# Grouped-query attention and a gated MLP on one core: idle matmuls with a bank of their own or not, normalisation without a DVE wait for the root, first-batch scores in pairs

## The chip, the core and the metric

The kernel runs on one NeuronCore of a Trainium2 chip. The core has a matrix engine (TensorE, PE in the profile; its weight loads are shown apart as PEld), and the engines VectorE (DVE), ScalarE (ACT), GpSimd (POOL) and SyncE (SP, which here issues transfers). Each engine runs its own queue strictly in the order written; they meet through semaphores. PE writes its results into PSUM, which has eight banks of 512 float32 values per partition. The metric is the device time of one execution in microseconds: 253.52 us before the change, the median of three runs (253.1, 253.52 and 254.39).

## What is computed

Attention over 8 batches with 16 query heads, 4 key/value heads, 384 positions and 64 values per head; its output goes as x (384 x 1024 per batch) into a gated MLP. The scores are so small that the kernel leaves out the subtraction of the maximum.

```python
scores = scale * np.matmul(q, k.transpose(0, 1, 3, 2))
attn = softmax(scores)                      # over keys
x = np.matmul(attn, v)                      # heads side by side: 1024 columns
h = np.maximum(x @ w_in, 0.0)               # 1024 x 1024
u, v = h[..., :512], h[..., 512:]
v_n = (v - mean(v)) / np.sqrt(var(v) + 1e-06)
v_s = np.einsum('ts,bsd->btd', w_spatial, v_n) + b_spatial[None, :, None]
out = (u * v_s) @ w_out
```

## The kernel before

The order of every engine's work is written out by hand: one loop over steps n (L594), where each step issues some of the following, in this order.

- `todo` entries (L595): loads, and casts of q, k and v on POOL to float16; from batch 2 on also transposes by DMA from SP.
- Scores (L597 to L601). A unit is one third of the keys for one group of query columns; a batch has 18 units. `scores(n)` issues two matmuls of a 64-row operand each (L233) and one exponential on ACT over both results (L240). In steps 0 to 16 one unit is issued a step, one step ahead; from step 18 on two units in every even step. The tile sc has two buffers, so a unit needs the exponential of the unit before last to be done.
- `weigh` (L242): every three units, 12 short matmuls (L247, four query tiles by three key tiles) into the tile av, twice, one step after the other. av has one buffer. DVE then takes the reciprocal of the sums (L257) and multiplies (L259) into x16; the next av waits for that.
- `turns` entries (L606): transposes on PE in the first batches (kps L188, qps L200, xps L275, each followed by a copy on DVE), and `keep_warm(4)` in steps 0 to 9, 14 and 15: four matmuls of an identity whose result nobody reads (L504). 27, 4 and 6 more stand ahead of step 0.
- `run_fill`: matmuls of the MLP from one generator (`stream`, L424), as many columns as the step is due. In batch 0 it gives work in steps 10 to 13 and from 16 on, none in 14 and 15. The MLP of a batch runs while the attention of the next one is issued; v_tile (pv, L294), u_tile or u_block (pu, L344 or L361), gate (psp, L380) and project (po, L406).

The tiles of the transposes, of the MLP and of the idle matmuls (`warm`) share the tag "ck" with three PSUM banks; sc takes four banks and av one. A ck tile takes the bank that was free longest; before the change `warm` is one tile that is made once (L500) and used last in step 15, so up to there the other ck tiles go round two banks, and a tile waits until the copy of the tile two before it is done.

The normalisation of a batch (`normal`, L311) comes in the middle of its u matmuls. DVE has clipped v into vr (L304) and taken statistics and mean and variance (L306, L307). ACT takes the logarithm of the variance and an exponential of -0.5 times that (L314, L315), which is the reciprocal root `rstd`. DVE multiplies minus the mean by it (`nmr`, L316), and POOL computes vn = vr * rstd + nmr three times (L322). psp reads vn. In the last batch no other attention is left beside this.

Of the kernel before, what the change touches and what calls it, by code (L numbers as in the profile page):

```python
# [9 lines left out]
FP32 = mybir.dt.float32  # L10
FP16 = mybir.dt.float16
AF = mybir.ActivationFunctionType
ALU = mybir.AluOpType
# [4 lines left out]
def kernel(  # L18
# [16 lines left out]
    nc = tc.nc  # L35
    P = 128
# [5 lines left out]
    NT = S // P  # L42
# [6 lines left out]
    NU = 18  # L49
# [7 lines left out]
    small = ctx.enter_context(tc.tile_pool(name="small", bufs=4))  # L57
# [3 lines left out]
    ps_ck = ctx.enter_context(tc.tile_pool(name="ps_ck", bufs=3, space=PSUM))  # L61
# [29 lines left out]
    def load_q0(j, lo, hi, eng):  # L91
# [18 lines left out]
            name=nc.get_next_instruction_name(), act_func_set_id=set_id, ins=[], outs=[]  # L110
# [113 lines left out]
    def scores(n):  # L224
        b, r = divmod(n, NU)
        m, t = divmod(r, NT)
        qt, j = divmod(m, 2)
        if t == 0:
            aTs[b, m] = att.tile([P, NT, 2, 512], FP16, name=f"aT_{b}_{m}", tag="aT", bufs=3)
        sc = ps_sc.tile([P, 2, 512], FP32, name=f"sc_{b}_{m}_{t}", tag="sc")  # L230
        for hh in range(2):
            half = slice(hh * D, (hh + 1) * D)
            nc.tensor.matmul(  # L233
                sc[:, hh],
                kTs[b][half, j, t * P : (t + 1) * P],
                qTs[b, j][half, qt],
                start=True,
                stop=True,
            )
        nc.scalar.activation(aTs[b, m][:, t], sc, AF.Exp, scale=scale)  # L240

    def weigh(b, m, hh):  # L242
        qt, j = divmod(m, 2)
        av = ps_av.tile([P, G, D + 1], FP32, name=f"av_{b}_{m}_{hh}", tag="av")
        for i in range(G):
            for t in range(NT):
                nc.tensor.matmul(  # L247
                    av[:, i, :],
                    aTs[b, m][:, t, hh, i * P : (i + 1) * P],
                    v1[b % 2][:, 2 * j + hh, t, 0 : D + 1],  # L250
                    start=(t == 0),
                    stop=(t == NT - 1),
                )
        if m == 0 and hh == 0:
            x16s[b] = att.tile([P, NT, NB, P], FP16, name=f"x16_{b}", tag="x16")
        r = small.tile([P, G, 1], FP32, name=f"r_{b}_{m}_{hh}", tag="r")
        nc.vector.reciprocal(r, av[:, :, D : D + 1])  # L257
        blk = 4 * j + 2 * hh
        nc.vector.tensor_tensor(  # L259
            x16s[b][:, qt, blk : blk + 2].rearrange("p k (i d) -> p (k i) d", i=2),  # L260
            av[:, :, 0:D],
            r.to_broadcast([P, G, D]),
            ALU.mult,
        )
# [21 lines left out]
    mvs, v_rs, v_ns, uTs, gTs, osbs = {}, {}, {}, {}, {}, {}  # L286
# [23 lines left out]

    def normal(b):  # L311
        rstd = small.tile([P, NT], FP32, name=f"rstd_{b}", tag="rstd")
        nmr = small.tile([P, NT], FP32, name=f"nmr_{b}", tag="nmr")
        nc.scalar.activation(rstd, mvs[b][:, :, 1], AF.Ln, bias=eps_t)  # L314
        nc.scalar.activation(rstd, rstd, AF.Exp, scale=-0.5)  # L315
        nc.vector.scalar_tensor_tensor(  # L316
            nmr, mvs[b][:, :, 0], -1.0, rstd, op0=ALU.mult, op1=ALU.mult
        )
        v_ns[b] = []
        for st in range(NT):  # L320
            vn = moe.tile([P, DH], FP16, name=f"vn_{b}_{st}", tag="vn", bufs=6)
            nc.gpsimd.tensor_scalar(  # L322
                vn,
                v_rs[b][st],
                rstd[:, st : st + 1],
                nmr[:, st : st + 1],
                op0=ALU.mult,
                op1=ALU.add,
            )
            v_ns[b].append(vn)  # L330

# [5 lines left out]
    def u_tile(b, st):  # L337

        pu = ps_ck.tile([P, NM, P], FP32, name=f"pu_{b}_{st}", tag="ck")
        for m in range(NM):  # L340
            for kt in range(NB):
                if st == 1 and m == 1 and kt == 0:
                    normal(b)
                nc.tensor.matmul(  # L344
                    pu[:, m],
                    w_in16[:, kt, m * P : (m + 1) * P],
                    x_tile(b)[:, st, kt],
                    start=(kt == 0),
                    stop=(kt == NB - 1),
                )  # L350
                if m < NM - 1 or kt < NB - 1:
                    yield P
        nc.vector.tensor_scalar(
            uT_tile(b)[:, :, st * P : (st + 1) * P], pu, 0.0, None, op0=ALU.max
        )
        yield P

    def u_block(b, m):
        pu = ps_ck.tile([P, 512], FP32, name=f"pu_{b}_{m}", tag="ck")
        for kt in range(NB):  # L360
            nc.tensor.matmul(  # L361
                pu[:, 0:S].rearrange("p (t s) -> p t s", t=NT),
                w_in16[:, kt, m * P : (m + 1) * P],
                x_tile(b)[:, :, kt],
                start=(kt == 0),
                stop=(kt == NB - 1),
            )
            if m == 0 and kt == 3:
                normal(b)
            if kt < NB - 1:  # L370
                yield S
        nc.scalar.activation(uT_tile(b)[:, m, :], pu[:, 0:S], AF.Relu)
        yield S
# [123 lines left out]

    by_dve, by_act = nc.vector.tensor_copy, nc.scalar.copy

    warm = ps_ck.tile([P, 512], FP32, name="warm", tag="ck")  # L500

    def keep_warm(n):
        for _ in range(n):
            nc.tensor.matmul(warm[:, 0:P], ident16, ident16, start=True, stop=True)  # L504

    keep_warm(27)
    cast_k(0, dve, (0,))
    cast_q(0, 0, dve, 0, 1, by_act)
    k_transposes(0, 0, by_dve)
    keep_warm(4)  # L510
    q_transposes(0, 0, 0, by_act, by_dve)
    keep_warm(6)
    scores(0)
    cast_k(0, pool, (1,))
# [71 lines left out]
    total = NU * B  # L586

    def run_fill(cols):
        nonlocal owed
        owed += cols  # L590
        while owed > 0:
            owed -= next(fill, 1e9)

    for n in range(total + 6):  # L594
        for f, args in todo.pop(n, []):  # L595
            f(*args)
        if n + 1 < NU:  # L597
            scores(n + 1)
        elif n >= NU and n % 2 == 0 and n < total:
            scores(n)  # L600
            scores(n + 1)  # L601
        for hh in range(2):
            b, r = divmod(n - 3 - hh, NU)
            if n >= 3 + hh and r % 3 == 0 and b < B:
                weigh(b, r // 3, hh)
        for f, args in turns.pop(n, []):  # L606
            f(*args)
        if n < NU + 3:

            run_fill(HV / 4 if 10 <= n < 14 else 2 * HV / 5 if 16 <= n else 0)  # L610
        elif n < 2 * NU + 4:
            run_fill((4 * HV + NM * NT * S + 6 * NM * 512) / (NU + 4 - 3))
        else:
            run_fill(COLS / NU)
# [31 lines left out]
```

## Time and profile before

| what | value |
|---|---|
| time, median of 3 runs | 253.52 us (253.1 to 254.39) |
| profiled execution, its own time | 253.12 us |
| span of the profiled execution | 251.3 us |
| PE busy | 240.9 us (96%) |
| ACT busy | 168.2 us (67%) |
| DVE busy | 139.7 us (56%) |
| POOL busy | 98.3 us (39%) |
| DVE idle ahead of nmr (L316), in all 8 | 9.9 us |
| PE idle, all stretches | 10.4 us |

Times in the profile are microseconds from the start of the span. A row of a timeline gives start, length, engine, line of the kernel, operation, tile written <- tiles read, shapes, and how many instructions are merged; a bracket names the idle time of that engine just before, and what ended it. Matmuls overlap in PE's pipeline, so the length of a row reaches past the start of the next one; what a piece of work costs PE is read from start to start. A row by stretch gives the busy time and number of instructions of PE, PEld, DVE, ACT and POOL, the granted clock, the busy share of the DMA engines and GB/s.

The matmuls run on PE at two speeds: the four idle matmuls at 4.80 us take 0.43 us start to start, those from 8.36 us on 0.22 to 0.24 us where no change to the 64-row form of the scores follows.

### The profile page before, as it was taken

The page shows a single profiled execution, that of the slowest core. Times are in us where ns is not written, and L with a number is a line of the kernel's source. Part 1 is how long each engine was busy: PE and PEld are TensorE (multiplying, and loading weights), DVE is VectorE, ACT ScalarE, POOL GpSimd, SP SyncE. Part 2 cuts the span into 40 slices and gives each one's busy share as a digit, 9 for nine tenths or more (in the row PEclk, how much of TensorE's full clock was granted, in tenths as well). Part 3 has the DMA queues.
Part 4 walks back from the last instruction along what each step waited for, and adds up shares of the span by engine and source line. Part 5 has one row for each costly group of instructions (what it writes and reads, how often), then busy time and mean ns, then how long its engine had stood idle before and what let it go on. Part 6 is the DMA issues. An engine that isn't in the chain of part 4 may idle for free.

```text
span 251.3 us, 6020 instructions
## 1 busy us (share of the span) xinstructions
PE 240.9 (96%) x2430; PEld 125.7 (50%) x2430; DVE 139.7 (56%) x368; ACT 168.2 (67%) x215; POOL 98.3 (39%) x142
## 2 busy tenths in 40 slices
PE   7898998999999999999999999999999999999883
PEld 7564657534455444544455445544455445544442
DVE  2455776854626755474626655474636655465462
ACT  3996566678696687768696687768696687741211
POOL 2698837871035701392036602391035003320320
PEclk9999999999999999999999999999999999999999
DMA  7999998999289964997399956997392452106006
GB/s 179 268 285 251 301 285 238 297 224 265 88 182 330 171 230 85 266 233 216 121 199 324 185 200 66 281 253 227 111 171 49 111 183 44 34 12 250 0 22 232
DMA packets 73981, 46.93 MB, mean 187 GB/s; under 512 B 48113, under 2 KB 68913, under 8 KB 73953
## 3 DMA queue, kind: packets, MB, share of 16 engines
q1 hardware_dynamic: 68832, 37.63, 59.4%
q0 software_dynamic: 4080, 8.65, 13.8%
q8 instruction: 19, 0.31, 0.5%
q10 hardware_dynamic: 1040, 0.26, 0.5%
q14 instruction: 10, 0.07, 0.1%
HBM read 25.95 MB, written 12.58 MB: 153 GB/s over the span
## 4 chain that ended last, share of the span: by engine, by line
PE 87%; DVE 7%; issue 1%; ACT 1%; POOL 1%; POOLq 0%; DVEq 0%
PE av L247 17%; PE pv L294 16%; PE sc L233 15%; PE po L406 15%; PE pu L361 13%; PE psp L380 6%; PE warm L504 3%; DVE stats L306 2%; DVE vr L304 2%; DVE x L259 2%; PE pu L344 1%; PE qps L200 1%; ACT aT L240 1%; POOL vn L322 1%; PE xps L275 1%
## 5 line engine op out<-in xcount | busy, mean ns | idle before, releaser
L240 ACT ACTIVATE aT<-sc 128x1024 f16<-128x1024 f32 x144 | 139.6, 1021 | 52.9 <-PE sc L233 52.7
L247 PEld LDWEIGHTS <-aT 128*128 128x128 f16 x1152 | 43.4, 97 | 32.9 <-DVE x L259 12.9
L322 POOL TENSOR_SCALAR vn<-vr,rstd,nmr 128x512 f16<-128x512 f32 x24 | 18.1, 767 | 99.6 <-DVE r L257 85.7
L247 PE MATMUL av<-v,aT 128*128 128x65 f16 x1152 | 52.3, 194 | 1.6 <-DVE x L259 1.2
L294 PE MATMUL pv<-w_in,xt 128*128 128x512 f16 x192 | 49.5, 378 | 0.0
L257 DVE RECIPROCAL r<-av 128x4 f32<-128x4 f32 x96 | 17.1, 178 | 58.3 <-PE av L247 57.8
L406 PE MATMUL po<-w_out,gT 128*128 128x512 f16 (+1 forms) x196 | 48.2, 375 | 0.9 <-POOL gT L392 0.9
L233 PE MATMUL sc<-qT,kT 64*128 64x512 f16 x288 | 45.0, 382 | 0.7 <-ACT aT L240 0.4
L259 DVE TENSOR_TENSOR x<-av,r 128x256 f16<-128x256 f32 x96 | 40.7, 424 | 3.4
L361 PE MATMUL pu<-xt,w_in 128*128 128x384 f16 x224 | 41.7, 326 | 0.0
L392 POOL TENSOR_TENSOR gT<-g,uT 128x384 f16<-128x384 f32 x30 | 26.5, 914 | 29.4 <-DVE g L390 29.4
L361 PEld LDWEIGHTS <-w_in 128*128 128x128 f16 x224 | 20.2, 97 | 14.7 <-issue 2.5
L406 PEld LDWEIGHTS <-gT 128*128 128x128 f16 x196 | 17.0, 97 | 19.4 <-issue 2.9
L170 POOL CAST q<-q 128x768 f16<-128x768 f32 (+1 forms) x36 | 24.9, 732 | 3.1 <-DMA q<-in_q_dram 3.1
L415 DVE COPY osb<-po 128x512 f32<-128x512 f32 (+1 forms) x25 | 16.8, 671 | 11.6 <-PE po L406 11.6
L294 PEld LDWEIGHTS <-xt 128*128 128x128 f16 x192 | 16.2, 97 | 13.5 <-issue 0.7
L415 ACT COPY osb<-po 128x512 f32<-128x512 f32 (+1 forms) x24 | 13.9, 580 | 12.4 <-PE po L406 12.3
L304 DVE TENSOR_SCALAR vr<-pv 128x512 f32<-128x512 f32 x24 | 16.5, 687 | 10.2 <-PE pv L294 10.0
L233 PEld LDWEIGHTS <-kT 64*128 64x128 f16 x288 | 8.9, 94 | 26.6 <-issue 24.4
L380 PE MATMUL psp<-wsT,vn 128*128 128x384 f16 x96 | 19.6, 326 | 0.6 <-POOL vn L322 0.6
L390 DVE TENSOR_TENSOR g<-psp,bias_b 128x384 f32<-128x384 f32 x32 | 16.4, 552 | 5.9 <-PE psp L380 5.9
L306 DVE BATCH_NORM_STATS2 stats<-vr 128x6 f32<-128x512 f32 x24 | 16.7, 695 | 0.8
(49 smaller groups left out, 125.8 us busy)
## 6 DMA issues: line engine op xcount, KB each, us to landing
out_dram<-osb SPq DMA_DIRECT2D x21, 512.0 KB, 2.9
q<-in_q_dram SPq DMA_DIRECT2D x10, 768.0 KB, 7.2
q<-in_q_dram POOLq DMA_DIRECT2D x4, 768.0 KB, 10.4
v<-in_v_dram SPq DMA_DIRECT2D x6, 384.0 KB, 8.7
w_in<-in_moe_w_in_dram POOLq DMA_DIRECT2D x4, 512.0 KB, 9.7
k<-in_k_dram SPq DMA_DIRECT2D x5, 384.0 KB, 4.2
out_dram<-osb SPq DMA_DIRECT2D x5, 256.0 KB, 2.0
q<-in_q_dram SPq DMA_DIRECT2D x2, 512.0 KB, 7.2
```

The lines of the kernel that those rows point to most:

```text
L170: f(q16s[b, j][:, lo:hi, :, hh, :], src[:, hh, lo:hi])
L233: nc.tensor.matmul(sc[:, hh], kTs[b][half, j, t * P : (t + 1) * P], qTs[b, j][half, qt], start=True, stop=True,)
L240: nc.scalar.activation(aTs[b, m][:, t], sc, AF.Exp, scale=scale)
L247: nc.tensor.matmul(av[:, i, :], aTs[b, m][:, t, hh, i * P : (i + 1) * P], v1[b % 2][:, 2 * j + hh, t, 0 : D + 1], start=(t == 0), stop=(t ...
L259: nc.vector.tensor_tensor(x16s[b][:, qt, blk : blk + 2].rearrange("p k (i d) -> p (k i) d", i=2), av[:, :, 0:D], r.to_broadcast([P, G, D]) ...
L294: nc.tensor.matmul(pv, x_tile(b)[:, st, kt], w_in16[:, kt, DH:DFF], start=(kt == 0), stop=(kt == NB - 1),)
L306: nc.vector.bn_stats(stats, vr)
L361: nc.tensor.matmul(pu[:, 0:S].rearrange("p (t s) -> p t s", t=NT), w_in16[:, kt, m * P : (m + 1) * P], x_tile(b)[:, :, kt], start=(kt == 0 ...
L380: nc.tensor.matmul(psp[:, 0:S], v_ns[b][st][:, m * P : (m + 1) * P], wsT16[:, st, :], start=(st == 0), stop=(st == NT - 1),)
L392: by.tensor_tensor(gTs[b][:, m, :], g, uTs[b][:, m, :], ALU.mult)
L406: nc.tensor.matmul(po[:, 0 : hi - lo], gTs[b][:, m, tt * P : (tt + 1) * P], w_out16[:, m, lo:hi], start=(m == 0), stop=(m == NM - 1),)
L415: (nc.scalar.copy if half and not i else nc.vector.tensor_copy)(osb[:, lo:hi], po[:, 0 : hi - lo])
```

## The change

Three edits:

1. `keep_warm` makes a new `warm` tile at each call, of the same tag. Between calls its bank goes back to the three that the ck tiles use in turn. The number of idle matmuls stays 85.
2. vn = (vr + minus) * rstd, where `minus` is minus the mean. DVE computes it from the mean alone; POOL waits for DVE and for ACT. nmr is gone.
3. In batch 0, units 0 to 12 are issued as before, no unit in step 12, unit 13 in step 13, and 14 with 15 and 16 with 17 in steps 14 and 16. From step 18 on nothing moves.

```diff
     def normal(b):
         rstd = small.tile([P, NT], FP32, name=f"rstd_{b}", tag="rstd")
-        nmr = small.tile([P, NT], FP32, name=f"nmr_{b}", tag="nmr")
+        minus = small.tile([P, NT], FP32, name=f"minus_{b}", tag="minus")
         nc.scalar.activation(rstd, mvs[b][:, :, 1], AF.Ln, bias=eps_t)
         nc.scalar.activation(rstd, rstd, AF.Exp, scale=-0.5)
-        nc.vector.scalar_tensor_tensor(
-            nmr, mvs[b][:, :, 0], -1.0, rstd, op0=ALU.mult, op1=ALU.mult
-        )
+        nc.vector.tensor_scalar(minus, mvs[b][:, :, 0], -1.0, None, op0=ALU.mult)
         v_ns[b] = []
         for st in range(NT):
             vn = moe.tile([P, DH], FP16, name=f"vn_{b}_{st}", tag="vn", bufs=6)
             nc.gpsimd.tensor_scalar(
                 vn,
                 v_rs[b][st],
+                minus[:, st : st + 1],
                 rstd[:, st : st + 1],
-                nmr[:, st : st + 1],
-                op0=ALU.mult,
-                op1=ALU.add,
+                op0=ALU.add,
+                op1=ALU.mult,
             )
             v_ns[b].append(vn)
...
-    warm = ps_ck.tile([P, 512], FP32, name="warm", tag="ck")
-
     def keep_warm(n):
+        warm = ps_ck.tile([P, 512], FP32, name="warm", tag="ck")
         for _ in range(n):
             nc.tensor.matmul(warm[:, 0:P], ident16, ident16, start=True, stop=True)
...
-        if n + 1 < NU:
+        if n < 12:
             scores(n + 1)
-        elif n >= NU and n % 2 == 0 and n < total:
+        elif n == 13:
+            scores(n)
+        elif n % 2 == 0 and n > 13 and n < total:
             scores(n)
             scores(n + 1)
```

## The prediction

> **What bounds the kernel now.** I read the shares first, then the chain that ended last, then busy time by stretch, then single engines in order of time where TensorE (PE) was idle. The page's shares, its 40 slices and its chain:
>
> ```profile
> PE 240.9 (96%) x2430; PEld 125.7 (50%) x2430; DVE 139.7 (56%) x368; ACT 168.2 (67%) x215; POOL 98.3 (39%) x142
> PE   7898998999999999999999999999999999999883
> PE 87%; DVE 7%; issue 1%; ACT 1%; POOL 1%; POOLq 0%; DVEq 0%
> ```
>
> PE bounds the span; at most the idle 10.4 us and what hides inside groups counted as busy can be won. Busy time by stretch says where it idles:
>
> ```profile
> 20.00:25.00 5.00, 4.16 (x61) 2.41 (x58) 3.31 (x9) 3.19 (x5) 3.91 (x6) 1.00 1.17 234
> 35.00:40.00 5.00, 4.43 (x70) 3.06 (x67) 3.37 (x10) 3.37 (x6) 0.63 (x1) 1.00 1.05 332
> 121.00:149.00 28.00, 27.97 (x274) 13.64 (x272) 15.50 (x42) 20.82 (x27) 10.60 (x14) 1.00 0.83 204
> 235.00:240.00 5.00, 4.37 (x27) 2.34 (x25) 1.65 (x4) 1.52 (x5) 3.15 (x4) 1.00 0.02 3
> ```
>
> The second number is PE. A middle batch (121 to 149) leaves it 0.03 us; the first batch (0.84 and 0.57 us idle in these two stretches) and the end (0.63) leave more. In order of time, PE in the first batch:
>
> ```profile
> 19.36 0.39 PE L233 MATMUL sc<-qT,kT 64*128 64x512 f16 x2
> 20.07 0.39 PE L200 MATMUL qps<-ident,q 128*128 128x128 f16 x4
> 21.29 0.38 PE L275 MATMUL xps<-ident,x 128*128 128x128 f16 x4 [0.84 <-DVE qT L205]
> 26.71 1.67 PE L294 MATMUL pv<-w_in,xt 128*128 128x512 f16 x7
> 28.31 0.60 PE L233 MATMUL sc<-qT,kT 64*128 64x512 f16 x4
> 28.85 0.54 PE L247 MATMUL av<-v,aT 128*128 128x65 f16 x12
> ```
>
> Two things: xps waits for the copy of qT out of the bank that both use, and a pair of units costs 0.54 us start to start (28.31 to 28.85), a single one 0.32 (19.36 to 19.68). Next, DVE at the first batch's normalisation and in a middle batch, with the PE rows that hang on it:
>
> ```profile
> 39.10 0.16 DVE L316 SCALAR_TENSOR_TENSOR nmr<-mv,rstd 128x3 f32<-128x3 f32 x1 [0.60 <-ACT rstd L315]
> 39.87 0.55 PE L247 MATMUL av<-v,aT 128*128 128x65 f16 x12 [0.57 <-DVE x L259]
> 127.19 0.16 DVE L316 SCALAR_TENSOR_TENSOR nmr<-mv,rstd 128x3 f32<-128x3 f32 x1 [1.45 <-ACT rstd L315]
> 127.34 0.61 PE L233 MATMUL sc<-qT,kT 64*128 64x512 f16 x4
> 127.96 0.54 PE L247 MATMUL av<-v,aT 128*128 128x65 f16 x12
> ```
>
> While DVE waits for the root, the division of the weighted values (L257, L259) is queued behind it, and the one bank of av with it: PE loses 0.57 us once, and 0.62 - 0.54 = 0.08 us inside the pair at 127.34. Last, the end:
>
> ```profile
> 235.04 0.20 ACT L315 ACTIVATE rstd<-rstd 128x3 f32<-128x3 f32 x1
> 235.28 0.16 DVE L316 SCALAR_TENSOR_TENSOR nmr<-mv,rstd 128x3 f32<-128x3 f32 x1 [0.60 <-ACT rstd L315]
> 235.64 2.26 POOL L322 TENSOR_SCALAR vn<-vr,rstd,nmr 128x512 f16<-128x512 f32 x3 [13.84 <-PE pu L361]
> 237.96 0.82 PE L380 MATMUL psp<-wsT,vn 128*128 128x384 f16 x4 [0.41 <-POOL vn L322]
> ```
>
> Root, nmr, three vn and then PE, with nothing beside it.
>
> **Banks and pairs, first batch.** The same 85 idle matmuls are issued; their tile no longer holds one of three ck banks until step 15. The order of DVE, ACT, POOL and SP stays; on PE only the scores of units 13 to 17 move. In the built order qps of step 12 now takes the bank of an older qps, and xps that of an older xps whose copy ended at 18.0: nothing is left for xps to wait for. From step 16's query transposes on, each ck tile has the same predecessor in its bank as before. I walk PE from 19.25 (the pv pair at 18.82 takes 2 x 0.216) with start-to-start times of rows of before:
> - step 12: av 0.39, qps 0.22, xps 0.22, two pv 0.53: 20.61
> - step 13: unit 13 0.32, av 0.39, two pv 0.53: 21.85
> - step 14: units 14 and 15 0.54, four idle matmuls 0.24, kps 0.22: 22.85
> - step 15: av 0.39, idle 0.22, kps 0.22, qps 0.22, xps 0.32; step 16: units 16 and 17 0.54, av 0.39, qps 0.22: 25.37.
>
> Two stalls are new. The pair of step 14 has av of step 15 close behind, and no filling work between (the filler gives nothing in steps 14 and 15). ACT starts an exponential 0.43 after its unit (22.04 to 22.47), takes 1.02, and a waiting av goes on about 0.06 later (at 60.35 an av stretched to 0.64 resumed so after the exponential of 59.58). Unit 14 at 21.85 is ready at 23.30, its av resumes at 23.36 instead of 22.91: 0.45 lost. Unit 15 waits for the exponential of 13 (21.04 to 22.06) about 0.03. So pv of step 16 comes at 25.85, not 26.71: 0.86 gained. Bounds: the stall may be nothing (1.31 gained) or the whole 1.02 (0.29); I take the walk. Behind PE in that stall stand only transposes and scores, all of them in the walk; ACT, which feeds it, is not delayed.
>
> What is late next: the first u matmuls come at 28.8 instead of 29.67, and their weights, issued by POOL at 15.9 and 16.6 with at most 11.3 us to land, are there by 27.9. DVE's copies keep up: kT's copy starts 1.54 after vr (23.50 to 25.04) and vr now at 22.07, so the bank of step 15's qps is free at 23.95; qps comes at 24.16. POOL's casts for batch 2 come 1 us earlier and their loads (issued at 28.5 and 29.4, 13.1 and 13.9 to land) still lie ahead. SP's key and query transposes (from 46.87) follow an x of DVE at 41.1, which moves with PE.
>
> The new waits of PE for itself (a bank last written by an idle matmul) are long over but one: the second qps at 5.44 writes a bank whose idle matmul ends at 5.43. It heads the chain to the first exponential; 0 to 0.1, I take 0.05 lost.
>
> A rule speaks against the stall. PE idles 1.0 us from 20.29 to 21.29 in this trace, and the four xps after it still take 0.22 (21.29 to 21.51), as the four qps before it; 0.45 us should not slow the clock either. The Trainium skill ("TensorE: Matmul & The Clock Gate", Part 1) has the gate fall to half after about 3.4 us of idleness; by that too the stall costs its own length, and the trace's 1.0 us agrees.
>
> **DVE without the root.** Eight times nmr (160 ns) becomes minus, a one-input operation on 128x3; the nearest rows are nmr and a 59 ns fill, and the next instruction starts 0.08 after it (39.10 to 39.18), so between 0 and 0.08 counts; I take 0.08.
> - First batch: aggregation ends at 38.50, minus 38.53, reciprocal 38.61, x 38.82 to 39.24, av 39.30 instead of 39.87. PE's own work before it ends at about 39.14, so 0.57 is gained (at most 0.73, at least 0 if something else held DVE).
> - Middle batches: reciprocal can start when av of 125.89 is out, about 126.5 and not 127.27; then av follows the pair after 0.54. The same 0.62 stands in six batches (71.24, 99.29, 127.34, 155.40, 183.45, 211.50): 6 x 0.08 = 0.48. The bounds are 0 and 0.48.
> - Last batch: POOL waits for ACT (ends 235.24) directly. Hops in these rows are 0.04 to 0.20, so vn starts at 235.28 to 235.44 instead of 235.64: 0.20 to 0.36; I take 0.24. psp, g, gT and the projection hang on it in a row, so it reaches the end.
> - vn keeps its shape and two scalars: 767 ns, same price. Fourteen osb copies of DVE now name a wait for ACT that the root's wait used to cover; the ACT copy meant is four osb tiles old. A wait instruction takes 21 ns on DVE's queue: nothing if covered by DVE's idle time, 0.3 at worst.
>
> **Sum**: 0.86 + 0.57 + 0.48 + 0.24 - 0.05 = 2.10 us. The profiled execution took 253.12 us (span 251.3 and 1.8 around it): 251.0. The median of the runs shown is 0.40 above it; I take half of that and say 251.2.
>
> **Rivals.**
> - The first-batch time is taken back by a load or by ACT: then only DVE's part stays, 1.29 - 0.05: 251.9, with the offset 252.1. For: DMA share is 1.05 to 1.2 in these stretches and POOL waits for a w_in landing until 28.5. Against: the margins of 0.9 us above.
> - DVE's wait only moves (something else holds reciprocal, or PE's 0.08 is its own): gain 0.86 + 0.24 - 0.05 = 1.05: 252.1, with the offset 252.3. For: the 0.08 is inside a modelled group. Against: 0.57 is plain idle time.
> - Slower: the idle matmuls now go round three banks among waiting tiles, PE rests at each and its clock falls. At half clock (four idle matmuls take 0.43 at 4.80 to 5.23 and 0.22 later) the 19 us up to step 16 would lose up to 12: 263. It decides from 3.4 us of work done at half clock (2.1 + 1.3). Against: the transposes of before already cycle through two banks with no slow row after 6.8. The same page of the Trainium skill ("A second HAM failure mode: psum-queue depth-cycling") describes such a fall; the trace does not show it.
> - Banks don't change what xps waits for, so the edit does not do what it says: 0.86 turns to about -0.1, which is the first rival's time.
>
> **How the numbers follow.** Forecast 0.71; first rival with the last one 0.12; second 0.10; slower 0.07. Less than 0.5% (1.27 us) is about what this measurement can't tell from no change: the line is at 252.25. Below it lie 0.67 of the forecast (the runs shown spread by 1.3 us, so its tail does not) and 0.13 of the two middle cases: 0.80; within it the other 0.13; slower 0.07. The forecast's own range is 250.4 (all upper bounds) to 251.8; the first two rivals take the range to 252.8.
>
> **What would show it.** Right: xps of step 12 right behind qps with no wait; av of step 15 stretched to about 0.8; pv x7 near 25.9; no idle time of DVE for ACT rstd; av at about 38.4 where 39.87 stood, without its 0.57; pairs of 0.54 in all middle batches; vn near 0.15 after the root at the end. Wrong: idle matmuls at 0.43 after 7 us, an av stall over 1 us in steps 14 to 18, u waiting for DMA near 28.8, or reciprocals waiting elsewhere.

## The result and the profile after

The changed kernel takes 252.18 us (median, 251.61 to 252.72) against 253.54 us: the ratio is 0.9941, interval 0.9921 to 0.996, so 1.4 us less, between 1.0 and 2.0. The prediction said 251.2 within 250.4 to 252.8, faster. Direction and range hold; the gain is six tenths of the forecast 2.3 us (253.54 - 251.2). The range holds only by the part that the first two rivals had added: the forecast's own range ended at 251.8, and 252.18 lies nearest to the first rival's 252.1. That the number falls inside does not confirm the sum, so each term is read below from its own rows.

The profiled execution took 251.95 us, its span 250.2. From the page, the shares and the chain:

```profile
PE 240.4 (96%) x2430; PEld 125.8 (50%) x2430; DVE 140.3 (56%) x368; ACT 168.2 (67%) x215; POOL 98.2 (39%) x142
PE 85%; DVE 6%; DMA 2%; POOL 2%; issue 1%; ACT 1%; POOLq 0%; DVEq 0%
```

PE is still the bound, but a transfer, which held no share of the chain before, now holds 2%. PE in order of time, the answering rows of the changed kernel:

```profile
18.82 0.39 PE L233 MATMUL sc<-qT,kT 64*128 64x512 f16 x2
...
20.18 0.39 PE L275 MATMUL xps<-ident,x 128*128 128x128 f16 x4
...
23.16 0.23 PE L247 MATMUL av<-v,aT 128*128 128x65 f16 x2
23.68 0.49 PE L247 MATMUL av<-v,aT 128*128 128x65 f16 x10 [0.29 <-ACT aT L240]
...
26.07 1.67 PE L294 MATMUL pv<-w_in,xt 128*128 128x512 f16 x7
...
38.68 0.55 PE L247 MATMUL av<-v,aT 128*128 128x65 f16 x12
...
55.29 0.61 PE L233 MATMUL sc<-qT,kT 64*128 64x512 f16 x4 [0.43 <-DMA qT<-q]
...
126.50 0.61 PE L233 MATMUL sc<-qT,kT 64*128 64x512 f16 x4
127.04 0.54 PE L247 MATMUL av<-v,aT 128*128 128x65 f16 x12
```

xps has no wait; the av of step 15 stops inside itself for unit 14's exponential; the av that stood at 39.87 has no bracket; the pairs of the middle batches cost 0.54 us to the next av. The scores of step 36, batch 2's first, wait for a transposing transfer: that bracket is new. DVE at the normalisation, and the end:

```profile
37.91 0.17 DVE L316 TENSOR_SCALAR minus<-mv 128x3 f32<-128x3 f32 x1
37.98 0.17 DVE L257 RECIPROCAL r<-av 128x4 f32<-128x4 f32 x1
...
233.88 0.20 ACT L315 ACTIVATE rstd<-rstd 128x3 f32<-128x3 f32 x1
...
234.25 2.26 POOL L320 TENSOR_SCALAR vn<-vr,minus,rstd 128x512 f16<-128x512 f32 x3 [13.61 <-ACT rstd L315]
...
236.57 0.82 PE L378 MATMUL psp<-wsT,vn 128*128 128x384 f16 x4 [0.41 <-POOL vn L320]
```

Where the time went, each number the distance between the same two pieces of PE's work in the two profiled executions (the spans are 251.34 and 250.17 us):

| stretch | before | after | difference |
|---|---|---|---|
| span's start to unit 12's scores (step 11) | 18.50 | 18.82 | +0.32 |
| to step 16's pv | 8.21 | 7.25 | -0.96 |
| to the av after the first normalisation | 13.16 | 12.61 | -0.55 |
| to step 36's scores | 16.12 | 16.61 | +0.49 |
| to the pair in the first middle batch | 15.25 | 15.27 | +0.02 |
| to the av behind the pair of the sixth | 140.88 | 140.40 | -0.48 |
| to psp behind the last vn, near the end | 25.84 | 25.61 | -0.23 |
| to the end of the span | 13.38 | 13.60 | +0.22 |

The column sums to -1.17, the difference of the spans. The four gains that the prediction priced are all there on PE. A loss at step 36 stands against them, and one at each end of the span.

The loss at the start is about 0.14 us up to the first scores (6.43, before 6.29) and 0.20 at the second query transposes, which start at 10.74, right behind POOL's cast of queries that had waited for their load.

The loss at the end is as large as the gain just ahead of it. The last copy of the output, before and after:

```profile
247.52 0.42 DVE L415 COPY osb<-po 128x256 f32<-128x256 f32 x1 [0.18 <-PE po L406]
```

```profile
246.13 0.42 DVE L413 COPY osb<-po 128x256 f32<-128x256 f32 x1 [0.18 <-PE po L404]
```

It ends at 247.94 and at 246.55. From there to the time of the profiled execution it is 5.18 us before (253.12 - 247.94) and 5.40 after (251.95 - 246.55). In all nine profiles of kernels with the second edit (this one and those of the experiments) this tail is 5.40 to 5.44 us, in all four without it 5.17 to 5.21. So the second edit also adds 0.22 us behind the last copy. In the traces DVE's closing instruction (a drain) starts 0.44 to 0.47 us after the one that releases it with this edit, and 0.09 without; why is not shown.

### The profile page after: what moved, and what is told of

Same layout as the page of the kernel before. It is cut to its first block, busy times and chain, and to the rows that moved or that the text cites. A ratio compares the mean times of both kernels' runs of the same rounds, so it can differ in the third digit from the quotient of the medians.

```text
span 250.2 us, 6016 instructions
## 1 busy us (share of the span) xinstructions
PE 240.4 (96%) x2430; PEld 125.8 (50%) x2430; DVE 140.3 (56%) x368; ACT 168.2 (67%) x215; POOL 98.2 (39%) x142
## 4 chain that ended last, share of the span: by engine, by line
PE 85%; DVE 6%; DMA 2%; POOL 2%; issue 1%; ACT 1%; POOLq 0%; DVEq 0%
PE av L247 16%; PE pv L294 15%; PE sc L233 15%; PE po L404 14%; PE pu L359 13%; PE psp L378 5%; PE warm L501 3%; DMA qT<-q 2%; PE pu L342 2%; ACT aT L240 1%; DVE x L259 1%; DVE stats L306 1%; DVE vr L304 1%; POOL gT L390 1%; PE qps L200 1%
## 5 line engine op out<-in xcount | busy, mean ns | idle before, releaser
L320 POOL TENSOR_SCALAR vn<-vr,minus,rstd 128x512 f16<-128x512 f32 x24 | 18.1, 766 | 97.5 <-ACT rstd L315 97.5
L259 DVE TENSOR_TENSOR x<-av,r 128x256 f16<-128x256 f32 x96 | 40.7, 424 | 3.3
```

Of the source, the lines that this page charges most:

```text
L259: nc.vector.tensor_tensor(x16s[b][:, qt, blk : blk + 2].rearrange("p k (i d) -> p (k i) d", i=2), av[:, :, 0:D], r.to_broadcast([P, G, D]) ...
```

## Experiments

Two theories were to be told apart. A: the walk holds, and what PE wins ahead of step 36 is partly eaten there, as batch 2's transposed queries stand behind loads in SP's queue; the later start is no effect of the code. B: the freed bank itself costs time by new waits of PE, which is why unit 12 stands 0.32 us later.

### Each edit alone

The first edit alone on the kernel before:

```diff
-    warm = ps_ck.tile([P, 512], FP32, name="warm", tag="ck")
-
     def keep_warm(n):
+        warm = ps_ck.tile([P, 512], FP32, name="warm", tag="ck")
```

> The kernel before with the first edit alone (a new tile for the idle matmuls at each call). Theory A (the walk of the prediction holds, and what is won ahead of step 36 is partly eaten there by a wait for batch 2's transposed queries, because SP's queue is full): xps of step 12 follows qps without a wait, 1.0 us won there; about 0.2 lost in step 15, where the query transposes come to a bank whose key copy stands behind the statistics on DVE; at step 36 a wait for the transposed queries of 0.2 to 0.5. In all 0.3 to 0.6 us faster than before. Theory B (the freed bank brings new waits of PE for itself, which is why the changed kernel's first scores stand 0.14 us and its step 12 stands 0.33 us later than before): the first scores start near 6.43 and step 12's av 0.3 later again, in every run that has this edit and in none without it; under A these two numbers vary from run to run whatever the edit.

Measured: 252.73 us, ratio 0.9973 (0.9961 to 0.9985). Two rows of PE from its profile:

```profile
20.67 0.39 PE L275 MATMUL xps<-ident,x 128*128 128x128 f16 x4
...
56.43 0.61 PE L233 MATMUL sc<-qT,kT 64*128 64x512 f16 x4 [0.99 <-DMA qT<-q]
```

From unit 12 to step 16's pv it takes 7.20 us, 1.01 less than before: the bank alone gives all of that, and the 0.2 us that were expected to be lost in step 15 are not. The wait at step 36 takes 0.99 of it back here, more than the 0.2 to 0.5 expected, so these scores stand at 56.43, later than before (55.99): on SP the x transpose was issued 0.61 us earlier than before (40.52 for 41.13) but took 2.37 us and not 1.78, and the query transposes came 0.41 us later (50.27 for 49.86). The profiled execution of this kernel was its slowest (254.19); by the ratio 0.7 us of the gain are kept, and what its other executions lost at step 36 no trace shows.

The second edit alone:

```diff
-        nc.vector.scalar_tensor_tensor(
-            nmr, mvs[b][:, :, 0], -1.0, rstd, op0=ALU.mult, op1=ALU.mult
-        )
+        nc.vector.tensor_scalar(minus, mvs[b][:, :, 0], -1.0, None, op0=ALU.mult)
...
+                minus[:, st : st + 1],
                 rstd[:, st : st + 1],
-                nmr[:, st : st + 1],
-                op0=ALU.mult,
-                op1=ALU.add,
+                op0=ALU.add,
+                op1=ALU.mult,
```

> The kernel before with the second edit alone (minus the mean on DVE, POOL waits for the root). Theory A: 0.57 won at the first batch's normalisation, 0.08 in each of six middle batches, 0.23 at the end, 1.28 in all, less a part of the 0.57 (0.1 to 0.5) that is eaten at step 36: 0.8 to 1.2 us faster than before. The rival that DVE's wait only moves: nothing at 39.87 and in the pairs, 0.2 us faster at most.

Measured: 252.53 us, ratio 0.9964 (0.9952 to 0.9976), 0.9 us. Its profiled execution, the slowest of the five (252.84), shows all three gains: 0.56 at the first normalisation (12.60 from pv to that av, 13.16 before), 0.08 in each of the six pairs and 0.23 at the last normalisation. It also shows 0.43 lost at step 36 (the row below), 0.25 at the scores of 171.09, 0.22 behind the last copy and 0.07 up to unit 12, so that it is 0.28 us faster (253.12 - 252.84). What the other four executions lost no trace shows.

```profile
55.93 0.61 PE L233 MATMUL sc<-qT,kT 64*128 64x512 f16 x4 [0.36 <-DMA qT<-q]
```

So the wait at step 36 comes whichever of the two edits brings PE there sooner. It belongs to neither.

The third edit alone:

```diff
-        if n + 1 < NU:
+        if n < 12:
             scores(n + 1)
-        elif n >= NU and n % 2 == 0 and n < total:
+        elif n == 13:
+            scores(n)
+        elif n % 2 == 0 and n > 13 and n < total:
```

> The kernel before with the third edit alone (units 14 with 15 and 16 with 17). Theory A: the wait of xps for the copy of qT stays (1.0 us start to start), two changes between the forms of PE's operands fewer win 0.2 to 0.3, the av of step 15 waits 0.5 for the exponential of unit 14: between 0.2 faster and 0.3 slower than before, no difference by the times. The rival, that pairs are worth something on their own: 0.3 us or more faster, and no stall inside the av of step 15.

Measured: 253.56 us, ratio 0.9995 (0.9979 to 1.0011): no difference. PE's rows:

```profile
20.82 0.38 PE L275 MATMUL xps<-ident,x 128*128 128x128 f16 x4 [0.84 <-DVE qT L205]
...
24.32 0.49 PE L247 MATMUL av<-v,aT 128*128 128x65 f16 x10 [0.29 <-ACT aT L240]
```

xps waits as before, and the av of step 15 stops for the exponential. What the pairs save in changes of operand form is taken back, by that stall or by xps's wait: 8.25 us from unit 12 to pv, 8.21 before.

The first and second edits without the third, so the changed kernel with this undone:

```diff
-        if n < 12:
+        if n + 1 < NU:
             scores(n + 1)
-        elif n == 13:
-            scores(n)
-        elif n % 2 == 0 and n > 13 and n < total:
+        elif n >= NU and n % 2 == 0 and n < total:
```

> The changed kernel without its third edit (scores of the first batch one unit a step, as before). Theory A: the freed bank wins 1.0 us at step 12 and no av of step 15 waits, so PE stands where it stands in the changed kernel at step 18, to within 0.1 us; the wait at step 36 is the same, and the time is that of the changed kernel within 0.2 us (0.5 to 0.6% faster than before). If the pairs are needed for the gain: 0.3% or more slower than the changed kernel.

Measured: 251.99 us, ratio 0.9944 (0.9931 to 0.9956), the changed kernel's time. Its distance from unit 12 to pv is 7.21 (7.25 with the pairs): the pairs are worth nothing in either company.

### The wait at step 36

First, SP's queue, in the kernel before and then in the changed kernel: start and length of each issue (the two loads of q stand in one row). Before:

```profile
41.13 1.78 SPq L279 DMA_TRANSPOSE xt<-x  x1
43.04 0.49 SPq L79 DMA_DIRECT2D k<-in_k_dram  x1
43.65 1.06 SPq L85 DMA_DIRECT2D q<-in_q_dram  x2
44.81 1.95 SPq L82 DMA_DIRECT2D v<-in_v_dram  x1
46.87 2.88 SPq L208 DMA_TRANSPOSE kT<-k  x1
49.86 5.28 SPq L215 DMA_TRANSPOSE qT<-q  x2
```

The time that the two query transposes took from issue to landing, and the scores of step 36, in the kernel before:

```profile
DMA to landing us min/median/max: 3.8/4.9/5.9
```

```profile
55.99 0.61 PE L233 MATMUL sc<-qT,kT 64*128 64x512 f16 x4
```

SP's queue in the changed kernel:

```profile
39.93 1.34 SPq L279 DMA_TRANSPOSE xt<-x  x1
41.40 1.37 SPq L79 DMA_DIRECT2D k<-in_k_dram  x1
42.89 1.06 SPq L85 DMA_DIRECT2D q<-in_q_dram  x2
44.06 2.19 SPq L82 DMA_DIRECT2D v<-in_v_dram  x1
46.35 2.77 SPq L208 DMA_TRANSPOSE kT<-k  x1
49.22 5.29 SPq L215 DMA_TRANSPOSE qT<-q  x2
```

SP has no gap over 0.2 us in either. Its x transpose did come 1.20 us earlier with PE, as the prediction said; the query transposes only 0.64, since the four loads now took 4.85 us to issue (41.40 to 46.25) where they had taken 3.72 (43.04 to 46.76). The slower of the two query transposes lands 5.9 us after its issue in both traces. If that is the first of them (PE's bracket fits only that), its data are there at 55.8 before and at 55.1 after. In the changed kernel PE goes on 0.17 us behind that (55.29 after 55.12); by the same measure it could have gone on at 55.93 in the kernel before, where it came at 55.99. So it had less than 0.1 us to spare.

The changed kernel with batch 3's loads behind batch 2's transposes:

```diff
-                at(w0 - NU + 11, load_k, b)
-                at(w0 - NU + 11, load_q, b, 0)
-                at(w0 - NU + 11, load_q, b, 1)
-                at(w0 - NU + 11, load_v, b)
+                l0 = w0 - NU + (13 if b == 3 else 11)
+                at(l0, load_k, b)
+                at(l0, load_q, b, 0)
+                at(l0, load_q, b, 1)
+                at(l0, load_v, b)
```

> The changed kernel, and batch 3's four loads issued from SP in step 31 behind batch 2's query transposes, not in step 29 ahead of its key transposes. Theory A (SP's queue order is what delays the transposed queries): the key transposes start about 4.8 us earlier on SP, the first scores of batch 2 wait for no transfer, 0.4 to 0.5 us faster than the changed kernel, which makes 1.7 to 1.9 us against before. The rival (the transfers themselves are late, as the DMA engines are full there): the wait of 0.43 us stays or comes back at batch 3, and the time is that of the changed kernel.

Measured: 251.17 us, ratio 0.992 (0.9898 to 0.9941), against 0.9941 for the changed kernel. SP's queue and the scores of step 36:

```profile
41.41 1.83 SPq L208 DMA_TRANSPOSE kT<-k  x1
43.35 3.32 SPq L215 DMA_TRANSPOSE qT<-q  x2
46.76 0.85 SPq L79 DMA_DIRECT2D k<-in_k_dram  x1
```

```profile
54.47 0.60 PE L233 MATMUL sc<-qT,kT 64*128 64x512 f16 x4
```

The bracket is gone. The time is 1.0 us below the changed kernel's 252.18, twice what was expected; the profiles show 0.49 at step 36 and 0.33 by an earlier start (unit 12 at 18.49 for 18.82). The key transposes start 4.94 us earlier and both query transposes are issued by 46.7, where they had only begun at 49.2. From the first normalisation's av to step 36 it takes 16.12 us (54.47 - 38.35), as before the change. The rival, slow transfers in themselves, falls.

The same move on the kernel before, with the same diff:

> The kernel before with only batch 3's loads moved behind batch 2's query transposes. Theory A: the transposes are issued 4 us earlier, but PE did not wait for them in the kernel before, so the time is that of before within 0.3 us. The rival (moving the loads is worth 0.4 us by itself, for instance since it spreads the traffic): 0.4 us or more faster than before.

Measured: 253.24 us, ratio 0.9992 (0.9983 to 1.0001), no difference. In these kernels the order of SP costs only once PE is early.

### The stall in step 15

The changed kernel with units 13 and 14 as the pair:

```diff
         elif n == 13:
             scores(n)
-        elif n % 2 == 0 and n > 13 and n < total:
+            scores(n + 1)
+        elif n == 14:
+            scores(n + 1)
+        elif n % 2 == 0 and n > 15 and n < total:
```

> The changed kernel with units 13 and 14 as a pair in step 13, 15 alone in step 14, 16 and 17 as before. Theory A (SP's queue decides when batch 2's transposed queries are there, so what PE wins ahead of step 36 is eaten there): the av of step 15 waits 0.1 us or less in place of 0.45, step 16's pv matmuls stand 0.3 to 0.4 us earlier after the same start, and the wait at step 36 grows by most of that; against before 1.3 to 1.6 us faster, which the times can't tell from the changed kernel. The rival (the wait is a fixed 0.43 us of transfer): the 0.35 us arrive at the end, 1.7 us faster than before.

Measured: 252.34 us, ratio 0.9954 (0.9938 to 0.997). The step was expected to win 0.3 to 0.4 us ahead of pv and wins 0.08 (7.17 for 7.25): a miss. At step 36 PE still waits for the transfer, as under A:

```profile
55.30 0.61 PE L233 MATMUL sc<-qT,kT 64*128 64x512 f16 x4 [0.80 <-DMA qT<-q]
```

And with the loads of batch 3 moved as well (both diffs):

> The changed kernel with both: units 13 and 14 as a pair, and batch 3's loads behind batch 2's query transposes. Theory A: nothing waits at step 36, so the 0.35 us of the shorter stall now arrive: 0.3 to 0.4 us faster than the kernel with the loads moved alone (251.17), 250.7 to 250.9 us. If something else of the first batch is next to hold PE, the time stays at 251.2.

Measured: 251.48 us, ratio 0.9923 (0.9911 to 0.9935): nothing more than the move of the loads alone (251.17), and a miss against the 250.7 to 250.9 expected. PE in step 15 of this kernel:

```profile
23.20 0.68 PE L247 MATMUL av<-v,aT 128*128 128x65 f16 x12
...
24.16 0.38 PE L200 MATMUL qps<-ident,q 128*128 128x128 f16 x4
24.58 0.38 PE L275 MATMUL xps<-ident,x 128*128 128x128 f16 x4
```

av still takes 0.52 us to the next piece (0.39 undisturbed), and xps, which followed qps after 0.22 us, now follows after 0.42. The stall goes and a wait two pieces later takes most of it. What xps waits for was not tried. It starts 0.05 us behind DVE's copy of the transposed keys (24.20 to 24.53), which stands behind the statistics; that it waits for that copy's bank is argued, not shown.

### The start, and both kernels again

The changed kernel and the one with batch 3's loads moved were run again beside a third, in which the loads of batches 3 to 7 all come two steps later. The first two are the same code as above. The third's diff against the changed kernel:

```diff
-                at(w0 - NU + 11, load_k, b)
-                at(w0 - NU + 11, load_q, b, 0)
-                at(w0 - NU + 11, load_q, b, 1)
-                at(w0 - NU + 11, load_v, b)
+                at(w0 - NU + 13, load_k, b)
+                at(w0 - NU + 13, load_q, b, 0)
+                at(w0 - NU + 13, load_q, b, 1)
+                at(w0 - NU + 13, load_v, b)
```

> The changed kernel once more, on the chip of these runs. Under theory A the start of the first scores (6.43 in the first profile; 5.83 to 6.43 in the runs so far) and the DMA landings of the first 12 us vary without a cause in the code, so this profile shows another start, while the distance from unit 12's scores to step 16's pv matmuls is 7.25 again (8.21 before) and the first scores of batch 2 wait for a transfer by 0.3 to 0.9 us. If the start is a property of the code, the first scores stand at 6.43 again.

Measured: 251.80 us, ratio 0.994 (0.9927 to 0.9954). The first scores start at 6.12 in this profile (6.43 in the first), and the distance from unit 12 to pv is 7.25 again. PE reaches step 36 earlier and waits longer, here to the same moment as in the first profile:

```profile
55.29 0.61 PE L233 MATMUL sc<-qT,kT 64*128 64x512 f16 x4 [0.88 <-DMA qT<-q]
```

> The changed kernel with batch 3's loads moved, once more, beside the changed kernel on one chip: 0.8 to 1.1 us faster than it, 251.2 us; no wait at step 36. Its start of the first scores (5.93 in its first profile) is where it was if the start belongs to the code, and anywhere from 5.8 to 6.45 if not.

Measured: 251.42 us, ratio 0.9928 (0.9908 to 0.9948), 0.38 us less than the changed kernel beside it: right in sign, below the 0.8 to 1.1 expected, and the intervals overlap. No scores of step 36 wait. The first scores stand at 6.29 (5.93 in its first profile). This profiled execution took 253.65 us because of batch 0's query loads:

```profile
15.07 0.74 POOL L170 CAST q<-q 128x256 f16<-128x256 f32 x2 [3.75 <-DMA q<-in_q_dram]
15.87 0.40 PE L200 MATMUL qps<-ident,q 128*128 128x128 f16 x4 [1.40 <-POOL q L170]
```

POOL's cast, and PE's third transposes of the queries (qps) behind it, waited for batch 0's queries to land; the second ones had waited 0.81. In the earlier run of the same code the second ones waited 0.22 and the third ones not: the first 16 us vary by more than a microsecond with the landing of the first loads.

The start of the first scores lies between 5.83 and 6.43 us in the nine profiles with the first edit and differs for the same code; in the four without it lies between 6.25 and 6.36. It goes with the moment at which PE's matmuls change from 0.107 us start to start to 0.056. With the first and second edits alone that is before 4.8 us (the four idle matmuls at 4.73 take 0.23), and the first scores start at 5.83. In the changed kernel's first profile all idle matmuls up to 6.43 are still slow; with the first edit alone even the first scores are (0.97 us for the four at 6.43, where the changed kernel's take 0.54). Theory B asked for a start near 6.43 in every run with the edit; five of nine start earlier, so it falls. The 0.32 us that the changed kernel loses up to unit 12 are about 0.14 of this start and 0.20 of a load; four profiles without the edit are too few to say whether their narrower spread is chance.

> The changed kernel with the loads of batches 3 to 7 all two steps later, behind both query transposes of the batch before, where batch 3 alone was moved until now. Theory A (transposed queries are late where SP has loads queued ahead of them): no wait for them at step 36, and none at a later batch either, as in the runs where one stood near 172 us (0.42 and 1.30); at most 251.2 us, and its runs no wider apart than 0.4 us. If later loads come too late for the casts, POOL waits for them and the time goes over 251.5.

Measured: 251.15 us, ratio 0.9909 (0.9895 to 0.9924). No scores wait for a transfer; its profiled execution (251.95) again lost its time at the start (unit 12 at 19.34), the others took 251.0 to 251.22; so the four lie 0.95 us apart and not within the 0.4 expected. It beats the kernel before by 0.9%, the changed kernel beside it by 0.65 us in the medians, and here the two intervals do not overlap (0.9924 and 0.9927). The wait of scores for queries that stands near 172 us in two profiles without the move (0.42 us with the first edit alone, 1.30 with units 13 and 14 as the pair) is not in this one, nor the 0.25 us that the second edit alone lost there; it is not in most of the others either, so that what the move does at later batches stays open.

## Why the prediction was right, and where it was wrong

- **The bank.** Right: xps's wait is gone, 0.96 us from unit 12 to pv against 0.86 predicted for bank and pairs. The edit alone gives 1.01. The rival by which the bank does not free xps falls.
- **The pairs.** The walk had them, the stall of 0.45 us included, and it is seen as 23.68 - 23.16 = 0.52 from av's start to its third matmul, of which 0.06 is its own. By itself the edit is worth nothing (8.25 against 8.21; 7.25 against 7.21).
- **PE's wait for itself**, taken as 0.05 us: it is there and costs nothing. The third of the four qps matmuls comes 0.156 us behind the second (0.122 before), and the fourth makes it up (0.061 for 0.091).
- **DVE without the root.** Right in each term as far as PE goes: 0.55 for 0.57, 0.48 for 0.48, 0.23 for 0.24. That the last one "reaches the end" was wrong: it reaches the last copy, and the tail behind that is 0.22 longer in every profile with this edit. No term of the sum had this. The operation minus takes 0.17 us and the reciprocal starts 0.07 behind it (0.08 assumed). The rival that DVE's wait only moves falls.
- **The step that failed** is the sentence that SP's key and query transposes "follow an x of DVE at 41.1, which moves with PE". The first of the chain does (1.20 us); the rest is a queue without a gap whose loads took 1.13 us longer to issue, so the query transposes moved by 0.64. Measured from the first normalisation's av to step 36 it cost 0.49 us in the first profile and 0.95 in the second, and moving the loads removes the wait. The term was in no bound. The rows to see it were there: SP without a gap from 41.1 to 55.1, the query transpose issued at 49.86 and up to 5.9 us to land, PE there at 55.99, so at most 0.2 us of slack for 1.4 us of advance. The first rival, a load or ACT taking back the first-batch time, is the nearest to what happened: a transfer took back about half of it in the first profile, at another place than its "w_in landing". That the median comes out at this rival's 252.1 is in part luck, as the losses at the start and at the end have other sources.
- **The offset.** Half of the 0.40 us between profile and median was added. The medians of before lie at 253.3 to 253.54, the profile at 253.12, so the whole would have been closer.
- **The clock.** The rival that PE's clock falls did not come (the 12 us at which it was priced are not worked out from rows); no idle matmuls stand at 0.43 after 7 us, and the stall cost its own length. The Trainium skill's rule ("TensorE: Matmul & The Clock Gate", Part 1), that idleness has to last about 3.4 us, agrees with that 0.52 us stall; no run here has a rest of PE as long as 3.4 us after the start.

Put together, 0.86 + 0.57 + 0.48 + 0.24 - 0.05 was 2.10; measured 0.96 + 0.55 + 0.48 + 0.23 = 2.22, less 0.49 at step 36, less 0.32 at the start, which varies for the same code, less 0.22 behind the last copy, which comes with the second edit, and less 0.02 behind step 36: 1.17, the difference of the two profiled executions (253.12 - 251.95).

## What to carry to other kernels

When PE gets faster in one stage, walk every queue that feeds the next stage, the issuing queue of transfers too, and write down each one's slack in microseconds: a queue without gaps can move by less than its first entry (here 0.64 us for 1.20). Transfers that are needed soon belong ahead of loads for a later batch in the same queue; here the move cost nothing in the kernel before (ratio 0.9992) and showed its worth only once the engine that waits was early. Where a second wait stands close behind the one that is removed, the gain is what that second wait leaves: an advance of 1.19 us ahead of step 36 was 0.70 behind it, and one of 1.65 us in the second profile was 0.70 too. And follow a gain to the end of the execution: 0.23 us won at the last normalisation were lost again behind the last copy.

## What the runs showed of the hardware

- The issue of a transposing transfer on SP is not of one length. Over all profiles batch 2's two query transposes took 4.91 to 5.79 us behind the four loads and 3.27 to 3.99 ahead of them, the key transposes 2.73 to 2.91 and 1.21 to 1.83.
- The issue of the four loads took 3.68 to 4.31 us where the first started at 42.9 to 43.1 us (four profiles) and 4.55 to 4.85 where it started at 40.7 to 41.4 (four others). Which of them grew differed: k took 1.37 us in the changed kernel's first profile and 0.49 in its second, where the two loads of q took 2.24 and not 1.06. What sets these lengths was not tried.
- The moment at which PE reaches full speed lay between 4.7 us (four idle matmuls in 0.23 us at 4.73, first and second edit) and after 7.4 us (the three kps matmuls at 7.40 still take 0.25, units 13 and 14 as the pair with the loads moved), though PE's first matmul started at 1.62 or 1.63 in all. The start of the first scores differed with it for the same code (6.43 and 6.12; 5.93 and 6.29). The Trainium skill says that this moment varies from run to run ("TensorE: Matmul & The Clock Gate", Part 1), and these runs agree.
